# Attention and a gated MLP on one core: buffers of x and of its parts shared by both halves of the MLP, g loaded into the place of its low part

## The chip, the cores and the metric

The kernel runs on one core of a Trainium2 chip. The metric is the device time of one execution in microseconds (us); the median of three runs is given, and one further execution was profiled. TensorE does the matrix products, VectorE (DVE), ScalarE (ACT) and GpSimd (POOL) the elementwise work, SyncE (SP) issues the transfers between HBM and the on-chip memory SBUF. TensorE adds up in PSUM, of which the kernel has four tiles, `ps0` to `ps3`.

## What is computed

Attention with rotary positions, then two gated layers. Four batches, eight heads, 576 positions, head size 64, width 512:

```
attn_out = softmax(rot(q) @ rot(k).T / 8) @ v          # 4 x 8 x 576 x 64
x = attn_out, heads side by side                       # 4 x 576 x 512

h = gelu_tanh(x @ w_in)                                # 4 x 576 x 1024
u, v = h[..., :512], h[..., 512:]
v_n = layer_norm(v) * g_ln                             # over the 512
v_s = einsum('ts,bsd->btd', w_sg, v_n) + b_sg[:, None]
g = u * v_s
x2 = x + g @ w_out

gate = sigmoid(causal_conv5(x2, conv_w))               # 5 taps along the positions, zeros ahead
out = (gate * (x2 @ w_val)) @ w_out2
```

The results must be as exact as float32 products. So each operand of a product is split into a high part (a rounded copy) and a low part (what the rounding left), and a product is the sum of three: high x high, high x low, low x high.

## The kernel before

**Stages.** Attention runs over 16 pairs of heads (0 to 289 us). Each pair leaves its unnormalised result in a scratch array `xu_d` in HBM and the reciprocals of its sums in `r_d`. Then comes the first half of the MLP, `part_a(b)` for the batches 0 to 3, some 41 us each (289 to 454 us), and then the second half (454 to 615 us).

**First half.** `x_prep(b)` makes x of a batch, in four tiles of 128 of the 512 columns (x is kept transposed, 128 columns by 576 positions). For each tile: a load of `xu_d`, a load of the broadcast reciprocals into `rb` (two DMAs), the product on GpSimd, a store of x to `x_d`, a rounded copy to `XH` on ScalarE, and the low part `XL` = x - `XH` on VectorE. `XH` and `XL` exist once (four tiles each), so the copies for batch b + 1 wait until TensorE has read those of batch b. `part_a(b)` then runs three products on TensorE: x by w_in for v (L607, 60 matmuls, 13.7 us), x by w_in for u (L646, 96 matmuls, 12.7 us; `u_unit`), and the mixing along the positions with w_sg (L660 and L663, 14.8 us; `g_unit`). `XH` and `XL` are read by the first two, so what prepares the next batch has the third as its time. `g_unit` ends with `vs` on VectorE (L667), a product with u on GpSimd, and a store of g to `g_d` in HBM.

`x_prep(0)` and the loading of w_sg use two tiles `xs0`, `xs1`. `x_prep(1)` to `x_prep(3)` use four, `xs0`, `xs1` and the two `gst` tiles, one for each of the four tiles of x.

**Weights.** Weights arrive as 64-bit floats. `weight64` loads one (512 KB, into the single raw buffer `wr0` from the first half on), takes a step on ScalarE (L281) and four on VectorE (L282 to L288) to make float32 `wf`, a rounded copy on ScalarE and a low part on GpSimd. Twelve of these (w_out, w_val, w_out2, four each: `wo`, `wv`, `wq`) are spread over the first half. The last is in place at 460.4 us.

**Second half.** When the first half's last work is done (`opened["2"]`, `close_a`), its pools are closed and the second half's tiles are put in their place. `load_g(b)` brings g of a batch back: a load into a staging tile (`gst`, for two tiles of batch 1 the `ob` tiles), a rounded copy to `gh` on ScalarE, the low part `gl` on VectorE. There are two sets `gh0`/`gl0` and `gh1`/`gl1`, for even and odd batches. `load_g(0)` runs in the first half, `load_g(1)` after `close_a`. `x2_part(b)`: for each of four tiles a load of x from `x_d` into one of four `x2` tiles (four zero columns and 576), 24 matmuls g by w_out (L728), an addition on VectorE into the `x2` tile (L734, this also frees the PSUM tile), a rounded copy `xh` on ScalarE, the low part `xl` on GpSimd, and the convolution `gt`: one ScalarE step (L743), four VectorE steps (L746), a sigmoid on ScalarE (L748). `val_part(b)`: four times 24 matmuls x2 by w_val (L761), a product with the gate on VectorE (L768), the split into `yh` and `yl`. `out_part(b)`: y by w_out2 (L790) and the output. The order on TensorE is `x2_part(0)`, half of `x2_part(1)`, `val_part(0)`, the other half of `x2_part(1)`, `out_part(0)`, half of `x2_part(2)`, and so on. Products take the PSUM tiles in turn, so a product can start when the result four before it has been read.

**What sets the order.** The program is first written as a list of tasks with an engine, an estimated duration and the tiles read and written (`Plan.add`); `Plan.order` then makes a schedule from these estimates (earliest possible, the most urgent first), and instructions are issued in that order. TensorE's order is fixed. On each engine, and in SyncE's queue, instructions run strictly in order: one that waits holds all behind it.

Of the kernel before, what the change touches and what calls it, by code (L numbers as in the profile page):

```python
# [155 lines left out]
def mixer_kernel(ctx: ExitStack, tc: tile.TileContext, qk, v, vrem, cs, w_in, g_ln, w_sgT, b_sg,  # L156
# [148 lines left out]
    def weights_a():  # L305
# [11 lines left out]
        for k in range(5):  # L317
            xs = XS[k % 2]
# [369 lines left out]

    def load_g(b):
        j = b % 2  # L690
        op = [opened["2" if j else "1"]]
        for k in range(4):
            y = k % 2
            spare = b == 1 and k > 1

            def st(y=y, spare=spare):
                return T["ob"][y].rearrange("p a b -> p (a b)")[:, 0:S] if spare else T["gst"][y]
            ks = ("ob" if spare else "gst", y)
            dma(290, lambda q, k=k, st=st: q.dma_start(out=st(), in_=g_d[b][128 * k:128 * k + 128, :]),
                [("g_d", b, k)], [ks], after=op)  # L700
            split(lambda k=k: T["gh"][j][:, k], lambda k=k: T["gl_"][j][:, k], st, S, [ks],
                  ("G", j, k, "h"), ("G", j, k, "l"), "D")
# [6 lines left out]
    def x2_part(b, dds=range(4)):  # L709
        j = b % 2  # L710
        op2 = [opened["2"]]
        for dd in dds:
            dc = slice(128 * dd, 128 * dd + 128)
            y = nx[0] % 4
            nx[0] += 1
            kx = ("x2", y)

            def x2(y=y):
                return T["x2"][y]
            dma(290, lambda q, dd=dd, x2=x2: q.dma_start(out=x2()[:, 4:S + 4], in_=x_d[4 * b + dd]),  # L720
                [("x_d", 4 * b + dd)], [kx], after=op2)
# [8 lines left out]
            ps, kp = unit(24 * PASS, mm, [("G", j, k, m) for k in range(4) for m in "hl"] + [(f"wo{k}", m) for k in range(4) for m in "hl"])  # L730

            def mid(x2=x2):
# [3 lines left out]
                [kp, ("x2z",)], [kx], after=op2)  # L736
# [107 lines left out]
    def close_a():  # L844
# [3 lines left out]
        T["gh"].append(p2.tile([128, 4, S], F32R, name="gh1"))  # L848
        T["gl_"].append(p2.tile([128, 4, S], F32R, name="gl1"))
# [6 lines left out]
        T["x2"] = [p2.tile([128, S + 4], F32, name=f"x2{j}") for j in range(4)]  # L856
# [7 lines left out]
    add("Pool", 0.3, lambda: [nc.gpsimd.memset(T["x2"][j][:, 0:4], 0.0) for j in range(4)], w=[("x2z",)], after=[opened["2"]])  # L864
# [74 lines left out]
```

## Time and profile before

| | us |
|---|---|
| median of three runs | 616.0 |
| lowest, highest | 615.06, 620.21 |
| the profiled execution | 616.6 |
| its span in the trace | 614.8 |
| TensorE busy | 579.0 (94%) |
| VectorE busy | 396.1 (64%) |
| ScalarE busy | 275.3 (45%) |
| GpSimd busy | 299.2 (49%) |
| granted TensorE clock, mean | 0.997 |

Times in the trace count from the span's start. The span is from the first to the last instruction; 1.8 us of the execution lie around it. TensorE's busy time is the union of its matmuls, whose ends are modelled. The trace names a wait by the instruction that ended it; "issue" stands where it names none.

### The profile page before, as it was taken

To read this page: it belongs to the slowest core of one execution; us is meant where nothing else is said; L and a number is where in the kernel's file an instruction comes from. 1 tells how busy PE (TensorE), PEld (TensorE's weight loads), DVE (VectorE), ACT (ScalarE), POOL (GpSimd) and SP (SyncE) were. 2 spreads that over 40 slices of the span, in tenths; PEclk is the share of its full clock that TensorE was granted. 3 is DMA by queue.
4 is the path that set the end of the run, shared out by engine and by line. 5 is a ranking of instruction groups with operands and counts; after the bars stand their busy time and mean duration, and the time that the engine had idled before them with its cause. 6 is when DMAs were issued, how large, how long until landed. Compare 5 with 4: busy or idle time off the path is not lost.

```text
span 614.8 us, 12049 instructions
## 1 busy us (share of the span) xinstructions
PE 579.0 (94%) x4648; PEld 465.5 (76%) x4648; DVE 396.1 (64%) x580; ACT 275.3 (45%) x447; POOL 299.2 (49%) x240
## 2 busy tenths in 40 slices
PE   1689999999999999999999999999998899999997
PEld 1456565666666566665899998998998889989985
DVE  5767765676666686771465666776457998938730
ACT  2426555555555556665441432624316554333321
POOL 6646565555555455556777745745544222201200
PEclk9989999999999999999999999999999999999999
DMA  7523644444444623665647246222144243130002
GB/s 254 166 83 86 182 144 123 124 118 128 122 100 130 190 74 111 194 198 141 197 143 278 76 154 218 79 97 85 38 150 155 78 138 124 39 125 2 35 31 90
DMA packets 54873, 76.80 MB, mean 125 GB/s; under 512 B 26528, under 2 KB 30624, under 8 KB 54816
## 3 DMA queue, kind: packets, MB, share of 16 engines
q1 hardware_dynamic: 54592, 76.03, 40.5%
q8 instruction: 36, 0.59, 0.4%
q14 instruction: 21, 0.17, 0.1%
q10 hardware_dynamic: 224, 0.00, 0.0%
HBM read 55.33 MB, written 18.95 MB: 121 GB/s over the span
## 4 chain that ended last, share of the span: by engine, by line
PE 80%; DVE 9%; DMA 7%; SPq 1%; POOL 1%; issue 1%; ACT 1%; DVEq 0%; ACTq 0%; POOLq 0%
PE ps L424 10%; PE ps L607 9%; PE ps L455 9%; PE ps L646 8%; PE ps L660 8%; PE ps L790 8%; PE ps L761 7%; PE ps L728 5%; PE ps L382 5%; PE ps L491 4%; DMA raw<-qk 3%; PE ps L432 3%; DVE mx L384 3%; DVE raw L236 2%; DVE gt L746 2%; PE ps L465 1%
## 5 line engine op out<-in xcount | busy, mean ns | idle before, releaser
L384 DVE TENSOR_REDUCE mx<-ps 128x2 f32<-128x576 f32 x128 | 96.2, 756 | 67.1 <-PE ps L382 66.5
L437 ACT ACTIVATE e<-ps 128x576 f32<-128x576 f32 x144 | 87.2, 648 | 70.0 <-PE ps L424 44.4
L455 PE MATMUL ps<-e,vm 128*64 128x288 f32 x512 | 77.6, 425 | 0.0
L382 PE MATMUL ps<-kh,qp 64*128 64x288 f32 x256 | 50.4, 393 | 24.1 <-ACT kh L240 13.0
L237 POOL TENSOR_TENSOR xl<-x,xh 128x576 fp32r<-128x576 f32 x16 | 27.9, 1751 | 88.1 <-ACT xh L240 79.4
L382 PEld LDWEIGHTS ps<-kh,qp 64*128 64x128 f32 x256 | 25.5, 197 | 56.6 <-DVE mx L384 23.1
L237 POOL TENSOR_TENSOR ac<-e,e 128x576 f32<-128x576 f32 x32 | 48.8, 1545 | 28.8 <-PE ps L491 27.0
L746 DVE SCALAR_TENSOR_TENSOR gt<-x,cw,gt 128x576 f32<-128x576 f32 x64 | 59.4, 967 | 3.5 <-ACT gt L743 3.2
L236 DVE TENSOR_TENSOR raw<-raw,cst 128x576 f32<-128x576 f32 x60 | 52.4, 888 | 8.1 <-DMA raw<-qk 8.1
L660 PE MATMUL ps<-s_h,vn 128*128 128x288 f32 x256 | 56.0, 294 | 0.0
L237 POOL TENSOR_TENSOR raw<-raw 128x576 f32<-128x576 f32 x30 | 43.4, 1446 | 16.8 <-DVE raw L236 15.1
L455 PEld LDWEIGHTS ps<-e,vm 128*64 128x64 f32 x512 | 31.3, 137 | 22.9 <-issue 6.0
L424 PE MATMUL ps<-qh,kh 64*128 64x288 f32 x256 | 42.0, 322 | 2.8 <-DVE mn L392 1.8
L660 PEld LDWEIGHTS ps<-s_h,vn 128*128 128x128 f32 x256 | 42.8, 188 | 0.0
L424 PE MATMUL ps<-mr,one_r 64*128 64x288 f32 x256 | 40.1, 302 | 0.1
L424 PE MATMUL ps<-qh,kl 64*128 64x288 f32 x256 | 39.4, 301 | 0.6 <-DVE kl L236 0.6
L761 PE MATMUL ps<-xh,wh_v 128*128 128x288 f32 x128 | 37.8, 295 | 1.8 <-DVE x L734 1.8
L424 PE MATMUL ps<-ql,kh 64*128 64x288 f32 x256 | 39.3, 300 | 0.0
L728 PE MATMUL ps<-gh,wh_o 128*128 128x288 f32 x128 | 37.7, 295 | 1.0 <-issue 1.0
L761 PE MATMUL ps<-xl,wh_v 128*128 128x288 f32 x128 | 37.8, 295 | 0.7 <-POOL xl L237 0.7
L237 POOL TENSOR_TENSOR vs<-vs,u 128x576 f32<-128x576 f32 x16 | 26.0, 1624 | 24.4 <-DVE vs L667 24.2
L660 PE MATMUL ps<-s_l,vn 128*128 128x288 f32 x128 | 37.8, 295 | 0.0
(145 smaller groups left out, 1576.2 us busy)
## 6 DMA issues: line engine op xcount, KB each, us to landing
raw<-qk SPq DMA_DIRECT2D x32, 576.0 KB, 4.5
xu_d<-xu SPq DMA_DIRECT2D x32, 144.0 KB, 3.4
rb<-r_d SPq DMA_DIRECT2D x32, 144.0 KB, 3.4
g_d<-vs SPq DMA_DIRECT2D x16, 288.0 KB, 2.7
x<-x_d SPq DMA_DIRECT2D x16, 288.0 KB, 2.9
vm<-v SPq DMA_DIRECT2D x16, 256.0 KB, 3.0
wr<-w_in SPq DMA_DIRECT2D x8, 512.0 KB, 5.5
wr<-w_out SPq DMA_DIRECT2D x8, 512.0 KB, 3.9
```

The costliest lines, as they stand in the source:

```text
L236: return add("DVE", dve(n), lambda: nc.vector.tensor_tensor(out_(), a(), b(), op), r, w, lock=True)
L237: return add("Pool", pool(n), lambda: nc.gpsimd.tensor_tensor(out_(), a(), b(), op), r, w, lock=True)
L382: nc.tensor.matmul(ps[:, h, 0:HALF], QP[j2][rows, c], kh[rows, cols], start=True, stop=True)
L384: add("DVE", 0.76, lambda: nc.vector.tensor_reduce(out=MX[j2][:, hk, :, c], in_=ps[:, :, 0:HALF], axis=AX.X, op=ALU.max), [kps], [("mx", j ...
L424: nc.tensor.matmul(ps[:, h, 0:HALF], x[rows, keys] if o < 3 else x[rows], y[rows, cols], start=o == 0, stop=o == 3)
L437: add("Act", 0.62, lambda: nc.scalar.activation(E[n], ps[:, :, 0:HALF], AF.Exp), [kps], [("e", n)])
L455: nc.tensor.matmul(pv[64 * hf:64 * hf + 64, h, 0:HALF], VM[j2][:, j, h], E[EU[i, us[hf]]][:, h], start=j == 0, stop=False, skip_group_chec ...
L607: nc.tensor.matmul(ps[:, y], X[p][:, k, o:o + 128], Wm[q][:, k, 512:1024], start=k == z == 0, stop=k == 3 and z == 2)
L660: nc.tensor.matmul(ps[:, hf, 0:HALF], VN()[p][:, k, dc], SG[q][:, k, cols], start=k == z == 0, stop=False)
L728: nc.tensor.matmul(ps[:, hf, 0:HALF], w2("o", p)[:, k, dc], (T["gh"], T["gl_"])[q][j][:, k, cols], start=k == z == 0, stop=k == 3 and z == 2)
L746: add("DVE", dve(S) + 0.05, lambda dd=dd, m=m, x2=x2, gt=gt: nc.vector.scalar_tensor_tensor(gt(), x2()[:, m:m + S], cw[:, 5 * dd + m:5 * d ...
L761: nc.tensor.matmul(ps[:, hf, 0:HALF], w2("v", p)[:, k, dc], (T["xh2"], T["xl2"])[q][j][:, k, cols], start=k == z == 0, stop=k == 3 and z == 2)
```

## The change

Four things are changed.

- `XH` and `XL`, the two tiles `xs` and the two tiles `rb` move from the first half's pool to the pool that lives through the whole kernel. `xs` and `rb` get four more columns in front, filled with zeros at the start on GpSimd; the first half uses columns 4 to 579.
- `x_prep(1)` to `x_prep(3)` use two tiles, `xs0` and `xs1`, each twice, as `x_prep(0)` does. The `gst` tiles are gone.
- `XH` and `XL` are `gh1` and `gl1` in the second half. `load_g` has no staging tile: g is loaded into the place of its own low part (`gl0`, or `XL`), copied from there to the high part, and the subtraction writes over its own input. It waits only for the tiles (and for `opened["1"]`), not for `close_a`.
- The four `x2` tiles are `xs0`, `xs1`, `rb0`, `rb1`. Their loads and the addition on VectorE no longer wait for `close_a`; the zero columns are not filled again.

```diff
+    XH = const.tile([128, 4, S], F32R, name="XH")
+    XL = const.tile([128, 4, S], F32R, name="XL")
+    XS = tiles(const, "xs", 2, [128, 4 + S], F32)
+    RB = tiles(const, "rb", 2, [128, 4 + S], F32)
-    XH = pA.tile([128, 4, S], F32R, name="XH")
-    XL = pA.tile([128, 4, S], F32R, name="XL")
-    XS = tiles(pA, "xs", 2, [128, S], F32)
-    RB = tiles(pA, "rb", 2, [128, S], F32)
...
+            for t in (*XS, *RB):
+                nc.gpsimd.memset(t[:, 0:4], 0.0)
...
     def x_prep(b):
-            y = hp if b else hp % 2
-            rb = RB[hp % 2]
-            kx = ("xs", y) if y < 2 else ("gst", y - 2)
-            op = [opened["1"]] if y > 1 else [at[13]]
+            y = hp % 2
+            rb = RB[hp % 2][:, 4:]
+            kx = ("xs", y)
+            op = [at[13]]
...
+    def gk(j, k, m):
+        return ("X", k, m) if j else ("G", k, m)
     def load_g(b):
         j = b % 2
-        op = [opened["2" if j else "1"]]
         for k in range(4):
-            y = k % 2
-            spare = b == 1 and k > 1
-            def st(y=y, spare=spare):
-                return T["ob"][y].rearrange("p a b -> p (a b)")[:, 0:S] if spare else T["gst"][y]
-            ks = ("ob" if spare else "gst", y)
-            dma(290, lambda q, k=k, st=st: q.dma_start(out=st(), in_=g_d[b][128 * k:128 * k + 128, :]),
-                [("g_d", b, k)], [ks], after=op)
-            split(lambda k=k: T["gh"][j][:, k], lambda k=k: T["gl_"][j][:, k], st, S, [ks],
-                  ("G", j, k, "h"), ("G", j, k, "l"), "D")
+            def g(k=k):
+                return T["gl_"][j][:, k].bitcast(F32)
+            kh, kl = gk(j, k, "h"), gk(j, k, "l")
+            dma(290, lambda q, k=k, g=g: q.dma_start(out=g(), in_=g_d[b][128 * k:128 * k + 128, :]), [("g_d", b, k)], [kl],
+                after=[opened["1"]])
+            acopy(lambda k=k: T["gh"][j][:, k], g, S, [kl], [kh])
+            tt("D", lambda k=k: T["gl_"][j][:, k], g, lambda k=k: T["gh"][j][:, k].bitcast(F32), ALU.subtract, S, [kh], [kl])
...
     def x2_part(b, dds=range(4)):
-        op2 = [opened["2"]]
-            y = nx[0] % 4
+            x2t, kx = ((XS[0], ("xs", 0)), (XS[1], ("xs", 1)), (RB[0], ("rb", 0)), (RB[1], ("rb", 1)))[nx[0] % 4]
...
             dma(290, lambda q, dd=dd, x2=x2: q.dma_start(out=x2()[:, 4:S + 4], in_=x_d[4 * b + dd]),
-                [("x_d", 4 * b + dd)], [kx], after=op2)
+                [("x_d", 4 * b + dd)], [kx])
...
-                [kp, ("x2z",)], [kx], after=op2)
+                [kp], [kx])
...
-        T["gst"] = [p1.tile([128, S], F32, name=f"gst{j}") for j in range(2)]
+        T["gh"] = [p1.tile([128, 4, S], F32R, name="gh0"), XH]
+        T["gl_"] = [p1.tile([128, 4, S], F32R, name="gl0"), XL]
...
-    add("Pool", 0.3, lambda: [nc.gpsimd.memset(T["x2"][j][:, 0:4], 0.0) for j in range(4)], w=[("x2z",)], after=[opened["2"]])
```

The planner makes a new order from this. TensorE's order and everything up to the middle of the first block of the MLP stay as they are. Three places follow.

VectorE, at the end of the block of batch 1 (after the weight conversion that stands there); `XL` rows are the low parts of x for batch 2, `vs` rows the `g_unit` of batch 1. Before:

```order
L236 TENSOR_TENSOR XL_136<-xs0_137,XH_135 128x576
L236 TENSOR_TENSOR XL_136<-xs1_138,XH_135 128x576
L236 TENSOR_TENSOR XL_136<-gst0_3322,XH_135 128x576
L236 TENSOR_TENSOR XL_136<-gst1_3323,XH_135 128x576
L667 SCALAR_TENSOR_TENSOR vs0_3333<-ps2_123,gsb_125,bsb_126 128x576
```

And now:

```order
L238 TENSOR_TENSOR XL_132<-xs0_133,XH_131 128x576
L238 TENSOR_TENSOR XL_132<-xs1_134,XH_131 128x576
L671 SCALAR_TENSOR_TENSOR vs0_3335<-ps2_123,gsb_125,bsb_126 128x576
L671 SCALAR_TENSOR_TENSOR vs1_3336<-ps3_124,gsb_125,bsb_126 128x576
L238 TENSOR_TENSOR XL_132<-xs0_133,XH_131 128x576
L286 TENSOR_SCALAR wt0_143<-wt0_143 128x512
L238 TENSOR_TENSOR XL_132<-xs1_134,XH_131 128x576
```

The third and fourth low part moved behind two `vs` steps and one weight step; the tiles they read are the first two's, loaded anew.

SyncE, around the same place: loads of x for batch 2 (`xu_d8` to `xu_d11`). Before, all four stand early, in the block of batch 0 (`g_d0` is the store of g of batch 0):

```order
L584 DMA xs0_137<-xu_d8_77 128x576
L299 DMA wr0_141<-w_out 128x1024
L584 DMA xs1_138<-xu_d9_78 128x576
L584 DMA gst1_3323<-xu_d11_80 128x576
L584 DMA gst0_3322<-xu_d10_79 128x576
L670 DMA g_d0_117<-vs0_3333 128x576
L588 DMA rb0_139<-r_d10_111 64x576 x2
```

And now, for the third and fourth (the loads of `xu_d8` and `xu_d9` stand a few rows further ahead, between the stores of `g_d0`):

```order
L595 DMA x_d8_93<-xs0_133 128x576
L592 DMA rb0_135<-r_d10_111 64x576 x2
L595 DMA x_d9_94<-xs1_134 128x576
L592 DMA rb1_136<-r_d11_112 64x576 x2
L674 DMA g_d0_117<-vs1_3336 128x576
L702 DMA gl0_3325<-g_d0_117 128x576
L303 DMA wr0_141<-w_out 128x1024
L303 DMA wr0_141<-w_val 128x1024
L588 DMA xs0_133<-xu_d10_79 128x576
L588 DMA xs1_134<-xu_d11_80 128x576
```

The loads of `xu_d10` and `xu_d11` moved behind the weights `wo3` and `wv0`, into the tiles that the first two leave.

VectorE, where the second half begins: `wt`, `wf` are steps of the last weight, `vs1_...<-ps3` the last step of the first half, `gl1` or `XL_132<-XL_132` the low parts of g of batch 1, L734 (L735 now) the additions of `x2_part(0)`, L746 (L747 now) convolution steps. Before:

```order
L667 SCALAR_TENSOR_TENSOR vs1_3334<-ps3_124,gsb_125,bsb_126 128x576
L282 TENSOR_SCALAR wt0_143<-wt0_143 128x512
L284 TENSOR_SCALAR wt0_143<-wt0_143 128x512
L286 SCALAR_TENSOR_TENSOR wt0_143<-wr0_141,wt0_143 128x512
L288 SCALAR_TENSOR_TENSOR wf0_142<-wr0_141,wt0_143 128x512
L236 TENSOR_TENSOR gl1_4848<-gst0_3322,gh1_4847 128x576
L236 TENSOR_TENSOR gl1_4848<-gst1_3323,gh1_4847 128x576
L236 TENSOR_TENSOR gl1_4848<-ob0_4865,gh1_4847 128x576
L236 TENSOR_TENSOR gl1_4848<-ob1_4866,gh1_4847 128x576
L734 TENSOR_TENSOR x20_4861<-ps0_121,x20_4861 128x576
L734 TENSOR_TENSOR x21_4862<-ps1_122,x21_4862 128x576
L734 TENSOR_TENSOR x22_4863<-ps2_123,x22_4863 128x576
```

And now:

```order
L238 TENSOR_TENSOR XL_132<-XL_132,XH_131 128x576
L671 SCALAR_TENSOR_TENSOR vs0_3335<-ps2_123,gsb_125,bsb_126 128x576
L238 TENSOR_TENSOR XL_132<-XL_132,XH_131 128x576 x2
L671 SCALAR_TENSOR_TENSOR vs1_3336<-ps3_124,gsb_125,bsb_126 128x576
L286 TENSOR_SCALAR wt0_143<-wt0_143 128x512
L288 TENSOR_SCALAR wt0_143<-wt0_143 128x512
L735 TENSOR_TENSOR xs0_133<-ps0_121,xs0_133 128x576
L290 SCALAR_TENSOR_TENSOR wt0_143<-wr0_141,wt0_143 128x512
L292 SCALAR_TENSOR_TENSOR wf0_142<-wr0_141,wt0_143 128x512
L735 TENSOR_TENSOR xs1_134<-ps1_122,xs1_134 128x576
L747 SCALAR_TENSOR_TENSOR gt0_4871<-xs0_133,cw_127,gt0_4871 128x576
L735 TENSOR_TENSOR rb0_135<-ps2_123,rb0_135 128x576
```

The low parts of g moved ahead of the last `vs` and the last weight, the first addition ahead of the end of that weight, and convolution steps stand between the additions.

## Rows read from the trace of the kernel before

**Rows 1.** TensorE's waits from 289 us on: waiting, releaser, us in total, times, longest.

```profile
PE ps L761 <- DVE x L734: 1.8, 1, 1.8
PE ps L728 <- issue: 1.0, 1, 1.0
PE ps L761 <- POOL xl L237: 0.7, 1, 0.7
```

**Rows 2.** Stretch, us, busy us (instructions) of PE PEld DVE ACT POOL, clock, DMA.

```profile
330.00:371.00 41.00, 41.00 (x268) 38.61 (x267) 25.54 (x40) 15.45 (x24) 27.40 (x22) 1.00 0.42 143
466.50:490.00 23.50, 20.07 (x148) 19.47 (x147) 22.77 (x26) 14.27 (x23) 10.47 (x6) 1.00 0.19 64
490.00:610.00 120.00, 120.00 (x744) 110.15 (x742) 77.92 (x112) 44.20 (x76) 17.43 (x10) 1.00 0.23 74
```

**Rows 3.** TensorE's timeline: start, us, what (idle before it and releaser in brackets).

```profile
466.38 0.29 PE L728 MATMUL ps<-gh,wl_o 128*128 128x288 f32 x1
```

**Rows 4.** The chain that ended last, in order of time: start, us, what.

```profile
371.56 13.65 PE ps L607 x60
...
483.32 6.62 PE ps L761 x48
489.94 6.36 PE ps L728 x48
```

**Rows 5.** VectorE's timeline, 454 to 481 us (columns as in rows 3).

```profile
454.05 0.82 DVE L667 SCALAR_TENSOR_TENSOR vs<-ps,gsb,bsb 128x576 f32<-128x576 f32 x1 [2.89 <-PE ps L663]
454.86 0.43 DVE L282 TENSOR_SCALAR wt<-wt 128x512 f32<-128x512 f32 x1
...
457.69 0.69 DVE L288 SCALAR_TENSOR_TENSOR wf<-wr,wt 128x512 int32<-128x512 int32 x1
...
466.79 0.76 DVE L734 TENSOR_TENSOR x<-ps,x 128x576 f32<-128x576 f32 x1 [1.17 <-DMA x<-x_d]
467.95 2.08 DVE L734 TENSOR_TENSOR x<-ps,x 128x576 f32<-128x576 f32 x3 [0.40 <-issue]
469.95 10.52 DVE L746 SCALAR_TENSOR_TENSOR gt<-x,cw,gt 128x576 f32<-128x576 f32 x9
```

**Rows 6.** GpSimd's timeline (columns as in rows 3).

```profile
9.79 5.05 POOL L237 TENSOR_TENSOR raw<-raw,cst 128x576 f32<-128x576 f32 x3 [5.38 <-DMA raw<-qk]
...
459.12 1.29 POOL L237 TENSOR_TENSOR wl_q<-wf,wh_q 128x512 fp32r<-128x512 f32 x1 [2.54 <-ACT wh_q L240]
...
469.05 7.16 POOL L237 TENSOR_TENSOR xl<-x,xh 128x576 fp32r<-128x576 f32 x4 [8.39 <-ACT xh L240]
```

**Rows 7.** SyncE: an issue of transfers, and a wait of its queue (400 to 500 us).

```profile
461.28 1.85 SPq L720 DMA_DIRECT2D x<-x_d  x4
SPq L670 <- POOL vs L237: 32.7, 8, 7.4
```

**Rows 8.** By tile, 455 to 500 us: durations min/median/max in ns.

```profile
L746 DVE SCALAR_TENSOR_TENSOR gt<-x,cw,gt x19: 800/806/2009, 469.9 to 497.2; 128x576 f32<-128x576 f32 x19
L237 POOL TENSOR_TENSOR xl<-x,xh x8: 1427/1910/1978, 469.1 to 498.1; 128x576 fp32r<-128x576 f32 x8
```

**Rows 9.** VectorE's timeline where batch 1 ends, low parts of x.

```profile
359.35 1.42 DVE L236 TENSOR_TENSOR XL<-gst,XH 128x576 fp32r<-128x576 f32 x2
...
364.19 0.82 DVE L667 SCALAR_TENSOR_TENSOR vs<-ps,gsb,bsb 128x576 f32<-128x576 f32 x1 [0.79 <-PE ps L663]
```

**Rows 10.** Tile xs, 285 to 500 us (ns; landing in us); weight loads, median us to landing.

```profile
L237 POOL TENSOR_TENSOR xs<-xs,rb x6: 1437/1600/1946, 298.7 to 366.9; 128x576 f32<-128x576 f32 x6
L240 ACT CAST XH<-xs x6: 665/672/681, 316.2 to 399.1; 128x576 fp32r<-128x576 f32 x6
L236 DVE TENSOR_TENSOR XL<-xs,XH x6: 751/754/757, 316.9 to 399.9; 128x576 fp32r<-128x576 f32 x6
DMA to landing us min/median/max: 2.6/3.5/5.6
wr<-w_out SPq DMA_DIRECT2D x8, 512.0 KB, 3.9
```

More of the change, by code (lines that the diff above doesn't have):

```diff
@@ L317, in weights_a @@
         for k in range(5):
-            xs = XS[k % 2]
+            xs = XS[k % 2][:, 4:]
             def ld(q, k=k, xs=xs):
@@ L576, in x_prep @@
             i = 4 * b + hp
-            y = hp if b else hp % 2
-            rb = RB[hp % 2]
-            kx = ("xs", y) if y < 2 else ("gst", y - 2)
-            op = [opened["1"]] if y > 1 else [at[13]]
+            y = hp % 2
+            rb = RB[hp % 2][:, 4:]
+            kx = ("xs", y)
+            op = [at[13]]
             def xs(y=y):
-                return XS[y] if y < 2 else T["gst"][y - 2]
+                return XS[y][:, 4:]
             dma(290, lambda q, xs=xs, i=i: q.dma_start(out=xs(), in_=xu_d[i]), [("xu_d", i)], [kx], after=op)
@@ L710, in x2_part, with x2 @@
         j = b % 2
-        op2 = [opened["2"]]
         for dd in dds:
             dc = slice(128 * dd, 128 * dd + 128)
-            y = nx[0] % 4
+            x2t, kx = ((XS[0], ("xs", 0)), (XS[1], ("xs", 1)), (RB[0], ("rb", 0)), (RB[1], ("rb", 1)))[nx[0] % 4]
             nx[0] += 1
-            kx = ("x2", y)
-            def x2(y=y):
-                return T["x2"][y]
+            def x2(x2t=x2t):
+                return x2t
             dma(290, lambda q, dd=dd, x2=x2: q.dma_start(out=x2()[:, 4:S + 4], in_=x_d[4 * b + dd]),
-                [("x_d", 4 * b + dd)], [kx], after=op2)
+                [("x_d", 4 * b + dd)], [kx])
             def mm(ps, dc=dc):
@@ L729, in mm @@
                                              start=k == z == 0, stop=k == 3 and z == 2)
-            ps, kp = unit(24 * PASS, mm, [("G", j, k, m) for k in range(4) for m in "hl"] + [(f"wo{k}", m) for k in range(4) for m in "hl"])
+            ps, kp = unit(24 * PASS, mm, [gk(j, k, m) for k in range(4) for m in "hl"] + [(f"wo{k}", m) for k in range(4) for m in "hl"])
             def mid(x2=x2):
@@ L743, in x2_part @@
             add("Act", act(S) + 0.09, lambda dd=dd, x2=x2, gt=gt: nc.scalar.activation(
-                gt(), x2()[:, 0:S], AF.Copy, scale=cw[:, 5 * dd:5 * dd + 1]), [kx, ("x2z",), ("cw",)], [kg])
+                gt(), x2()[:, 0:S], AF.Copy, scale=cw[:, 5 * dd:5 * dd + 1]), [kx, ("consts",), ("cw",)], [kg])
             for m in range(1, 5):
@@ L816, in close_att @@
             T["wl" + nm] = p1.tile([128, 4, DM], F32R, name=f"wl_{nm}")
-        T["gh"] = [p1.tile([128, 4, S], F32R, name="gh0")]
-        T["gl_"] = [p1.tile([128, 4, S], F32R, name="gl0")]
-        T["gst"] = [p1.tile([128, S], F32, name=f"gst{j}") for j in range(2)]
+        T["gh"] = [p1.tile([128, 4, S], F32R, name="gh0"), XH]
+        T["gl_"] = [p1.tile([128, 4, S], F32R, name="gl0"), XL]
         pa2 = stA2.enter_context(tc.tile_pool(name="pA2", side="right", bufs=1))
@@ L847, in close_a @@
         p2 = ctx.enter_context(tc.tile_pool(name="pB2", bufs=1))
-        T["gh"].append(p2.tile([128, 4, S], F32R, name="gh1"))
-        T["gl_"].append(p2.tile([128, 4, S], F32R, name="gl1"))
         for nm in ("xh2", "xl2"):
@@ L855, in close_a @@
         T["yr"] = [p2.tile([128, 2, 4, 128], F32R, name=f"yr{j}") for j in range(2)]
-        T["x2"] = [p2.tile([128, S + 4], F32, name=f"x2{j}") for j in range(4)]
         T["ob"] = [p2.tile([128, 2, 512], F32, name=f"ob{j}") for j in range(2)]
```

## Prediction

> **What bounds the kernel now.** I first read where TensorE waits, because it is busy 94% of the span. From 289 us to the end it waits three times only: 1.8 us for VectorE's `x`, 1.0 us for something unnamed, 0.7 us for GpSimd's `xl` [rows 1]. The table by stretch says the same from the other side: TensorE is busy 41.00 of 41.00 us in a block of the first MLP half and 120.00 of 120.00 us from 490 to 610, but only 20.07 of 23.50 us between 466.5 and 490 [rows 2]. So a change to the MLP can gain only in those 23.5 us, and it can lose wherever it makes TensorE wait elsewhere.
>
> How large that gain can be at most: the last matmul of `x2_part(0)` starts at 466.38 [rows 3] and the next would follow 0.13 later, at 466.51. From there to the end of `val_part(0)` stand six products of 24 matmuls; two of them take 6.36 us in the chain [rows 4], so 3.18 each and 19.08 together: 485.59 without any wait. In fact the chain has 483.32 + 6.62 = 489.94 [rows 4]. The ceiling is 4.35 us, of which 3.5 are the three waits of [rows 1] and the rest is restart.
>
> Why it waits there: the first half ends with the last weight. VectorE finishes its conversion at 457.69 + 0.69, ScalarE rounds it, GpSimd subtracts from 459.12 to 460.41 [rows 5, 6], and only then are the buffers of the second half handed out. The four `x` tiles are loaded from 461.28 on [rows 7], and VectorE's additions of `x` run at 466.79 and from 467.95 to 470.03 [rows 5], although the first of the four products had been ready since 466.51 − 3 × 3.18 = 456.97. Everything behind them is late by some 9 us: GpSimd's `xl` (469.05) [rows 6], VectorE's convolution (469.95, without a break until 480.47) [rows 5].
>
> **The change part by part.**
>
> *Buffers of x.* The `x2` tiles now are XS and RB, which exist all along. Their loads stand in SyncE's queue ahead of the last `g_d` stores, behind the end of `x_prep(3)`, so they land tens of microseconds before 457. The additions then follow TensorE: 457.3 (VectorE has a 1.54 us weight step up to there), 460.4, 463.6 and, since VectorE's queue is in order, 466.7 for the last, which ends at 467.4.
>
> *g in place of its low part, in XL and XH.* Loads, copies and subtractions stay 4 per batch, of the same size (ScalarE 0.67, VectorE 0.75, as for the parts of x [rows 10]), so they add no work. For batch 1 they move from behind the last weight to the 14.8 us in which TensorE runs `g_unit`, after `u_unit` releases XH and XL at about 439.1 (four products of 3.18 and the 14.7 of `g_unit` before 466.51). Four loads issued from 439.3 land by about 445 (four such `x` loads issued from 461.28 were all there by 467.95 [rows 5, 7]), and the four subtractions now stand between VectorE's `vs` steps and the last two weights. Their price: 4 × 0.75 = 3.0 us on VectorE, most of it in its pauses (2.89 us ahead of the last `vs` alone [rows 5]); what does not fit pushes the last conversion from 458.38 to about 459.4, and GpSimd's last weight step from 460.41 to about 461.5. So the second half's own buffers open 1.1 us later than before, but less hangs on them.
>
> *The convolution.* ScalarE starts `gt` at 461.5 and `xh` at 462.3; GpSimd's four `xl` run from 463.1 to 470.3. TensorE goes straight from 466.51 into batch 1 (ps0 is free since 458) and needs `xl` at 472.87: the wait of 0.7 us is gone with 2.6 us to spare. VectorE does two of its convolution steps before 467.4; eight follow before the gate product of the first `val` result. A step takes 0.81 us alone and up to 2.01 beside GpSimd, whose `xl` then takes 1.91 instead of 1.43 [rows 8]. With two held up by 1.1 and six at 0.8 they end at 475.9, and the first `val` product ends at 476.05. So the first late addition of batch 1, which frees ps0, ends at 477.8, before TensorE asks for it at 479.23: the wait of 1.8 us is gone too. The second one stands behind four more steps, of which one is held up by the next `xl`: it ends at 483.2, and TensorE asks for ps1 at 482.41. **One wait of 0.8 us is left.** Gain: 4.35 − 0.8 = **3.5 us**.
>
> What stands behind the rows on [rows 8] is stated by the Trainium skill, "SBUF — State Buffer", section "Who interferes with whom": a VectorE instruction with two SBUF inputs and a GpSimd instruction that reads SBUF exclude each other for a whole instruction. It speaks against this change, which brings subtractions under GpSimd's `vs` products; the trace agrees (2.01 against 0.81 us). Without such exclusion the left-over wait would be nil and the gain 4.3; with it, 3.5.
>
> *x_prep with two buffers instead of four.* Before, four tiles were loaded, multiplied and stored early, so that at the end of `u_unit` (356.72) four copies and four subtractions ran back to back, done at 359.35 + 1.42 = 360.77 [rows 9]. Now the second pair can only be loaded when VectorE's subtraction has released the first. Worked for block 1: subtraction of the first tile at 358.0, load issued at 358.8 (as SyncE did before for the next batch) and landed 3.5 us later, 362.3 [rows 10]; GpSimd has the `vs` product until 363.1, then two multiplications of 1.60 [rows 10], to 364.7 and 366.3; copy 0.67, subtraction behind `vs` of 364.19: 366.1; the last pair 367.0 and 367.7, with one weight step between. TensorE needs them at 371.56 [rows 4]: 3.9 us to spare, three times. The store to `x_d` and the loads of `rb` lie in SyncE's queue behind; nothing waits for them in this block. Cost on the path: **0**. If the cover is gone, each microsecond beyond 3.9 costs one at each of three block starts.
>
> *Small things.* Four GpSimd fills of four columns move to the start, where GpSimd is idle for 5.38 us before its first product, since a transfer is what it waits for [rows 6]: 0; only past 5.38 us would they delay it. `g` of batches 2 and 3 now loads only when TensorE has read the old values (466.5 and about 493), but is needed at 504 and 546: 0.
>
> **Sum.** 614.8 − 3.5 = 611.3 us of span; the profiled execution took 616.6, 1.8 more than its span, so 613.1. The median of the three runs, 616.0, lies 0.6 below that execution; against it the forecast is 616.0 − 3.5 = **612.5 us**, 0.6% faster. A measurement of this kernel can tell about 1% from no change, so this counts as "same".
>
> **Rivals.**
> *The wait only moves (616).* If VectorE is not ahead after all, TensorE stops at ps1 instead of ps0. It costs one for one from 482.41 on; the whole gain is lost when the second addition ends at 486.8, 3.6 us after my 483.2. That takes three more convolution steps held to 2.0 us, or buffers that open 3.6 us later since the last weight is late. For it: VectorE has no pause from 469.95 to 490 and is the engine that the longest wait names [rows 1, 5]. Against: its first addition moves 9 us forward and GpSimd's interfering products with it. 0.17.
>
> *Two buffers are too few (slower).* The chain subtraction, load, product, copy, subtraction must fit into `g_unit`'s 14.8 us. The slowest `xs` load seen took 5.6 us, 2.1 more than my 3.5 [rows 10]; that alone stays inside 3.9. If SyncE's queue, in order and with a weight load that waits for VectorE just ahead of the pair, holds it 3 us more, TensorE waits 1.2 us three times and the gain is spent: the kernel is slower than before from 5.1 us of lateness per block, 619 at 6.1. For it: one queue carries all this, and its waits for GpSimd's `vs` were up to 7.4 us [rows 7]. Against: the weight just ahead must be converted by 358.0; its load, after the conversion before it (about 345.4 in the new order), takes 3.9 [rows 10], ScalarE comes to it behind `u` at 351.1, and VectorE's four steps take 3.5 (454.86 to 458.38 [rows 5]) and a few tenths of waiting: 355.3. 0.10.
>
> *All of the 4.35 us (611.7).* The left-over 0.8 rests on one step held up by `xl`; where GpSimd starts a little later, nothing is left. This lies within the forecast's own range.
>
> **How the numbers follow.** Forecast (gain 2 to 4.35): 0.70; the wait moves (gain under 2): 0.17; X late: 0.10; other, as an effect of addresses or of the first half's shifted weight order: 0.03. Range: below, the ceiling of 4.35 and the scatter of the lower runs (615.06 is 0.9 below the median) give 610.8; above, the case without a gain, 616.5. Forecast's own range: 611.2 to 614.2. Faster by over 1% would need 6.2 us, more than the ceiling: 0.03. Slower by over 1% needs X to be late by (6.2 + 3.5) / 3 + 3.9 = 7.1 us in each block: 0.06. Within 1%: 0.91.
>
> **What would show it.** Right: from 289 us on TensorE waits once for under 1.5 us, at the last product of `val_part(0)`, with VectorE's addition as releaser; VectorE's first addition stands at about 457; 490 to the end is as dense as before, 3.5 us earlier. Wrong: a wait of `X Wm` products at a block start with `XL` or the `xs` load ahead of it; the last weight's GpSimd step well after 461.5; an addition into ps1 ending later than 484.

## The result and the profile after

The changed kernel takes 612.9 us (median), the kernel before 616.0 in the same comparison. The ratio is **0.9919, 95% interval 0.9894 to 0.9944**: 0.8% faster. That is the forecast case (612.5 us, 0.6% faster), and within 1%. The ratio's interval means 3.4 to 6.5 us on 616.0; the medians lie 3.1 us apart, the profiled spans, 614.8 and 611.1, 3.7. Single executions of one kernel scatter by more than that (608.3 to 618.2 for the changed one), so where the time went is read from the traces. Page of the changed kernel, span and busy times:

```profile
span 611.1 us, 12019 instructions
PE 580.7 (95%) x4648; PEld 467.1 (76%) x4648; DVE 389.2 (64%) x580; ACT 276.0 (45%) x447; POOL 301.1 (49%) x240
```

The list of TensorE's waits from 280 us on is now empty; the three of [rows 1] are gone (0.25 us that the list does not name is taken up under `short_xl`). The table by stretch (columns as in [rows 2]) shows the same for the 23.5 us in which TensorE was busy for 20.07 before:

```profile
330.00:371.00 41.00, 41.00 (x267) 38.36 (x266) 26.28 (x43) 16.56 (x27) 27.38 (x22) 1.00 0.55 182
466.50:490.00 23.50, 23.50 (x178) 23.28 (x177) 20.16 (x25) 13.96 (x24) 8.05 (x5) 1.00 0.32 102
```

Since lines were added, L607, L660, L728, L734, L746, L761, L768 and L790 of before are L611, L664, L729, L735, L747, L762, L769 and L791 after. The chain after (start, us, what), the products that answer to [rows 4] and a few more:

```profile
330.98 13.94 PE ps L611 x60
...
372.47 13.94 PE ps L611 x60
...
455.45 19.09 PE ps L729 x144
474.53 12.97 PE ps L762 x96
487.50 6.36 PE ps L729 x48
493.86 10.92 PE ps L791 x48
...
530.21 13.62 PE ps L791 x60
```

and of the kernel before, products by `w_h` and by `wh_q` that no group ahead shows:

```profile
330.36 13.65 PE ps L607 x60
...
496.30 11.20 PE ps L790 x48
532.94 13.94 PE ps L790 x60
```

The first product after the transition stands at 487.50 instead of 489.94 [rows 4], only 2.44 us earlier, although TensorE no longer waits. Two things that I had not worked out lie beside the transition: each block of the first half has become 0.29 us longer (L611: 13.94 against 13.65), and each output product shorter (L791: 10.92 against 11.20 for 48 matmuls, 13.62 against 13.94 for 60). I cut the trace of every kernel at the starts of matmuls: the first of the first block, the first of `x2_part(0)`, the first behind `val_part(0)`, and the end. These sums, in us, answer most of what follows (`only_x` and the rest are the kernels of the experiments below; each was profiled in one execution):

| kernel | four blocks | transition | rest | all three |
|---|---|---|---|---|
| before | 164.90 | 35.98 | 125.00 | 325.88 |
| changed | 166.08 | 32.05 | 123.72 | 321.85 |
| `only_x` | 164.91 | 36.73 | 123.68 | 325.32 |
| `only_g` | 164.91 | 33.18 | 125.00 | 323.09 |
| `two_buf` | 164.90 | 34.66 | 125.01 | 324.57 |
| `one_buf` | 205.20 | 31.81 | 123.71 | 360.72 |
| `pad_w` | 164.90 | 32.05 | 123.70 | 320.65 |
| `pad_w256` | 166.11 | 32.05 | 123.73 | 321.89 |
| `pad_w64` | 166.41 | 32.05 | 123.72 | 322.18 |
| `pad_before` | 164.91 | 35.26 | 123.70 | 323.87 |
| `short_xl` | 166.11 | 31.81 | 123.70 | 321.62 |

So from before to after: +1.18 in the blocks, -3.93 in the transition, -1.28 in the rest, -4.03 in all (and the first block began 0.31 later, which leaves the 3.7 of the two spans). What stands ahead of the first block, the attention, is left out of the table: over these eleven executions it ended anywhere from 287.2 to 293.2 us, in no order of the kernels. One execution of each kernel was profiled, so no run shows whether the change moves that end as well, nor how much of the scatter of the measured times it is.

### The profile page after: what moved, and what is told of

It is laid out like the page before. It is cut to its first block, busy times and chain, and to the rows that moved or that the text cites. A ratio compares the mean times of both kernels' runs of the same rounds, so it can differ in the third digit from the quotient of the medians.

```text
span 611.1 us, 12019 instructions
## 1 busy us (share of the span) xinstructions
PE 580.7 (95%) x4648; PEld 467.1 (76%) x4648; DVE 389.2 (64%) x580; ACT 276.0 (45%) x447; POOL 301.1 (49%) x240
## 4 chain that ended last, share of the span: by engine, by line
PE 84%; DVE 7%; DMA 5%; SPq 1%; issue 1%; ACT 1%; POOL 0%; DVEq 0%; ACTq 0%; POOLq 0%
PE ps L428 9%; PE ps L611 9%; PE ps L459 9%; PE ps L762 8%; PE ps L650 8%; PE ps L729 8%; PE ps L664 8%; PE ps L791 8%; PE ps L386 5%; PE ps L495 4%; PE ps L436 3%; DVE mx L388 3%; DVE raw L238 2%; DMA raw<-qk 2%; PE ps L667 1%; DMA rc<-ss 1%
## 5 line engine op out<-in xcount | busy, mean ns | idle before, releaser
L459 PE MATMUL ps<-e,vm 128*64 128x288 f32 x512 | 79.0, 431 | 0.0
L664 PE MATMUL ps<-s_h,vn 128*128 128x288 f32 x256 | 56.0, 294 | 0.0
L238 DVE TENSOR_TENSOR raw<-raw,cst 128x576 f32<-128x576 f32 x60 | 48.7, 826 | 6.9 <-DMA raw<-qk 6.9
L459 PEld LDWEIGHTS ps<-e,vm 128*64 128x64 f32 x512 | 31.8, 139 | 23.5 <-issue 7.0
L664 PEld LDWEIGHTS ps<-s_h,vn 128*128 128x128 f32 x256 | 42.7, 188 | 0.0
L239 POOL TENSOR_TENSOR kl<-raw,kh 128x576 fp32r<-128x576 f32 x15 | 22.6, 1508 | 31.6 <-ACT kh L242 30.8
L650 PE MATMUL ps<-XH,w_l 128*128 128x288 f32 x128 | 37.8, 295 | 0.0
L762 PE MATMUL ps<-xh,wh_v 128*128 128x288 f32 x128 | 37.8, 295 | 0.0
L762 PE MATMUL ps<-xh,wl_v 128*128 128x288 f32 x128 | 37.8, 295 | 0.0
L664 PE MATMUL ps<-s_l,vn 128*128 128x288 f32 x128 | 37.7, 295 | 0.0
L650 PE MATMUL ps<-XL,w_h 128*128 128x288 f32 x128 | 37.7, 294 | 0.0
```

The costliest lines, as they stand in the source:

```text
L238: return add("DVE", dve(n), lambda: nc.vector.tensor_tensor(out_(), a(), b(), op), r, w, lock=True)
L239: return add("Pool", pool(n), lambda: nc.gpsimd.tensor_tensor(out_(), a(), b(), op), r, w, lock=True)
L459: nc.tensor.matmul(pv[64 * hf:64 * hf + 64, h, 0:HALF], VM[j2][:, j, h], E[EU[i, us[hf]]][:, h], start=j == 0, stop=False, skip_group_chec ...
L650: nc.tensor.matmul(ps[:, hf, 0:HALF], Wm[p][:, k, dc], X[q][:, k, cols], start=k == z == 0, stop=k == 3 and z == 2)
L664: nc.tensor.matmul(ps[:, hf, 0:HALF], VN()[p][:, k, dc], SG[q][:, k, cols], start=k == z == 0, stop=False)
L762: nc.tensor.matmul(ps[:, hf, 0:HALF], w2("v", p)[:, k, dc], (T["xh2"], T["xl2"])[q][j][:, k, cols], start=k == z == 0, stop=k == 3 and z == 2)
```

## The experiments

The theory: TensorE's waits in the transition go because both loads, of x and of g, no longer stand behind the last weight. Rivals: the loads of x are all of it; or the buffers of `x_prep` are a loss that hides part of it. A second question came from the chain: what makes L611 and L791 change speed.

### Only the buffers of x2 (`only_x`)

The kernel before, with `XS` and `RB` as constant tiles used by `x2_part`; `load_g` and `x_prep` as before.

```diff
-            y = nx[0] % 4
-            kx = ("x2", y)
+            x2t, kx = ((XS[0], ("xs", 0)), (XS[1], ("xs", 1)), (RB[0], ("rb", 0)), (RB[1], ("rb", 1)))[nx[0] % 4]
...
-                [("x_d", 4 * b + dd)], [kx], after=op2)
+                [("x_d", 4 * b + dd)], [kx])
```

> One part of the change alone: x2_part works in the four buffers of x and r, so the loads of x stand ahead of the end of the first half; g still goes through gst and ob, after it, and x_prep keeps four buffers. Theory: both early loads are needed. The first additions come at about 457, 460, 463.6 and 466.7, but the four subtractions of g's low part (block 1) stand behind the fourth of them on VectorE, so they end at 470.3 (0.75 us each) to 473 (1.43 each beside POOL's xl), and the first product of x2_part(1), which reads them and is asked for at 466.5, waits 3.8 to 6.5 us; the later waits (0.69 and 1.76) go, since their work is then early. Against the 3.43 us of waits before that is 0.4 to 3 us worse. The distances of the tiles (theory A of the paddings) are 0 for both 512-column products, which gives 1.26 back: 615.2 to 617.9, centre 616. Rival: the loads of x are the whole effect; then no wait is left and the time is 616.0 - 4.1 - 1.3 = 610.6.

Measured: ratio to before 1.0022 (0.9997 to 1.0048), that is 617.4 us on 616.0, not told apart from the kernel before. The additions are early, but now TensorE's wait is for g: 2.8 us in two pieces, where I had expected 3.8 to 6.5 in one. Its list of waits, and VectorE's timeline (columns as in [rows 5]):

```profile
PE ps L729 <- DVE gl L237: 2.8, 2, 1.5
```

```profile
460.66 0.76 DVE L735 TENSOR_TENSOR xs<-ps,xs 128x576 f32<-128x576 f32 x1 [0.41 <-PE ps L729]
...
470.20 0.76 DVE L735 TENSOR_TENSOR rb<-ps,rb 128x576 f32<-128x576 f32 x1 [1.70 <-PE ps L729]
470.87 1.58 DVE L237 TENSOR_TENSOR gl<-gst,gh 128x576 fp32r<-128x576 f32 x2
472.37 2.63 DVE L237 TENSOR_TENSOR gl<-ob,gh 128x576 fp32r<-128x576 f32 x2
474.92 3.00 DVE L747 SCALAR_TENSOR_TENSOR gt<-xs,cw,gt 128x576 f32<-128x576 f32 x4
```

The four subtractions of g end at 475, behind the fourth addition, as expected. TensorE starts again after each of them in turn and stands twice for 1.5 us at most. Six products took 24.0 us where 19.1 is the length without waits, though the waits are only 2.8. The table by stretch tells a part of why:

```profile
471.00:475.00 4.00, 1.94 (x8) 1.47 (x9) 4.00 (x5) 2.11 (x4) 1.78 (x2) 0.88 0.46 149
475.00:478.00 3.00, 3.00 (x16) 3.00 (x16) 3.00 (x5) 2.71 (x4) 0.00 (x0) 0.60 0.02 6
478.00:481.30 3.30, 3.30 (x27) 3.30 (x27) 3.30 (x5) 0.63 (x2) 0.00 (x0) 1.00 0.32 89
```

TensorE was busy for 1.94 of 4.00 us, and then the granted clock was 0.60 over three microseconds (partly at the lower of its two levels, 1.2 GHz), in which 16 matmuls ran where 22 to 23 go at 0.133 us each: 0.9 us. The other 1.2 lie in longer distances between the matmuls around the two waits. The rival (no wait left, 610.6) is out, by the ratio and by the waits: the loads of x alone are worth nothing, as the work on g takes their place.

### Only g in its own place (`only_g`)

The kernel before, with `XH` and `XL` as constant tiles and the new `load_g`; `x2` has its own four tiles, opened by `close_a`.

```diff
-        op = [opened["2" if j else "1"]]
...
+                after=[opened["1"]])
...
-        T["gh"] = [p1.tile([128, 4, S], F32R, name="gh0")]
...
+        T["gh"] = [p1.tile([128, 4, S], F32R, name="gh0"), XH]
```

> The other part alone: g is loaded into XL's place and its high part into XH, early; x2_part has its own four tiles, opened at the end of the first half, and x_prep keeps four buffers. Theory: no subtraction of g is left in the transition and the loads of x are no longer behind two loads into ob; they are issued about 460.2 instead of 461.3 and the first addition comes at about 465.5, before TensorE asks for its buffer at 466.5, so the wait of 0.98 goes; the second addition of x2_part(1) ends about 484.2 where TensorE asks at 482.4, so one wait of about 1.8 is left of 3.43: 614.4 us. Both 512-column products keep their distances of before (0 and 128 mod 256), so L607 takes 13.65 and L790 13.94: no change from those. Rival: the loads of x are the whole effect, then all three waits stay and the time is 616.0.

Measured: ratio 0.9943 (0.9916 to 0.997), transition 33.18 us. One wait is left (`PE ps L761 <- DVE x L734: 1.1, 1, 1.1` in its list), where I expected 1.8. VectorE's timeline:

```profile
465.62 1.49 DVE L734 TENSOR_TENSOR x<-ps,x 128x576 f32<-128x576 f32 x2 [5.09 <-DMA x<-x_d]
...
481.59 0.74 DVE L734 TENSOR_TENSOR x<-ps,x 128x576 f32<-128x576 f32 x1
...
483.71 0.75 DVE L734 TENSOR_TENSOR x<-ps,x 128x576 f32<-128x576 f32 x1
```

VectorE stands idle for 5.09 us until x has landed; its first addition comes at 465.6, which is 463.8 in the time of before, since the transition began at 455.67 here and at 453.80 there. I had expected 465.5, which was 1.7 too late. The addition that TensorE waits for is the first late one, into ps0: it ends at 482.33, and TensorE's next product starts at 482.39. I had expected the second, into ps1, to be the one that counts; behind the wait at ps0 that one (ended at 484.46) is in time. So the first wait goes as expected, the place of the last was wrong, and the price 0.7 less. In all, g is the larger part: 2.8 us of the 3.9 against the profile of before. The early loads of x add 1.13 to it, but only on top of it. The two parts are not a sum: 36.73 and 33.18 alone, 32.05 together, from 35.98.

### Only two buffers in `x_prep` (`two_buf`)

The kernel before with this one edit:

```diff
-            y = hp if b else hp % 2
+            y = hp % 2
```

> The kernel before with one edit: x_prep uses two buffers of x for every block instead of four (gst stays for g alone). Theory: a block's XL is ready about 3 us before its first product also with two buffers (368 against 371.6), so the time stays at 616.0 and no wait stands ahead of L607. Rival (two are too few): the third and fourth load come behind the release of the first two, XL ends after 371.6, and each of the three later blocks loses up to 3 us: 619 to 625.

Measured: ratio 0.9978 (0.9945 to 1.0012), four blocks 164.90 us as before to a hundredth. No wait stands at a block's start; two buffers cost nothing. In the transition, which this edit leaves alone, two of the three waits stand as before:

```profile
PE ps L761 <- DVE x L734: 1.8, 1, 1.8
PE ps L761 <- POOL xl L237: 0.6, 1, 0.6
```

The unnamed one of 1.0 is not there. In `pad_before`, whose transition is also that of before, it was 0.3:

```profile
PE ps L730 <- issue: 0.3, 1, 0.3
```

The first of the four loads of x took 5.4 us from issue to landing in the profile of before, 4.7 in `pad_before` and 4.1 in `two_buf`. So this wait depends on when x lands in one execution: the transition of before took 35.98, 35.26 and 34.66 us in the three, 35.3 in the mean, and against that mean 0.7 of the 3.9 us gained were the profiled execution's own.

### One buffer of x (`one_buf`)

The changed kernel with this one edit:

```diff
-            y = hp % 2
+            y = 0
```

> The changed kernel with one buffer of x in x_prep instead of two (the two of r stay). It shows where the spare time of 3.1 us ends. Theory: a pair must then be loaded (2.6 to 3.5 us), multiplied (1.4), stored and split before the next is loaded, about 6.5 us a pair; only the first is ready when u_part frees XH, so the fourth XL comes about 6 to 8 us after TensorE asks for it in each of the three later blocks: 612.9 + 18 to 24, about 632 us, with waits of DVE XL ahead of L611. Rival (x_prep has more slack than that, since work of the block before covers it): under 2 us a block, below 619.

Measured: 654.4 us in one run; the blocks take 205.20 us, 39.1 more than in the changed kernel, 13 for each of the three later blocks. The pair's cycle is longer than I put it: for the second block the last two products on GpSimd follow one another by 8.58 us (335.76 to 344.34), not 6.5, and I had expected about 632 us.

```profile
PE ps L611 <- ACT XH L242: 28.9, 6, 7.9
```

```profile
335.76 1.87 POOL L239 TENSOR_TENSOR xs<-xs,rb 128x576 f32<-128x576 f32 x1 [3.48 <-DMA xs<-xu_d]
344.34 1.40 POOL L239 TENSOR_TENSOR xs<-xs,rb 128x576 f32<-128x576 f32 x1
```

```profile
333.40:347.00 13.60, 4.14 (x12) 2.30 (x11) 6.73 (x10) 4.45 (x7) 5.85 (x4) 0.66 0.81 263
347.00:360.70 13.70, 13.70 (x51) 10.81 (x50) 8.69 (x22) 5.64 (x8) 6.66 (x6) 0.84 0.48 138
```

The waits are 28.9 of the 39.1. Of the other 10.2, about 8.5 are matmuls that follow one another more slowly; the granted clock was 0.66 in the stretch in which TensorE stood and 0.84 in the one behind. The remaining 1.7 lie in the first intervals after the waits. So the rival "two buffers are too few" had the right mechanism and the wrong count: one buffer fewer turns 3 us to spare into 13 us of loss a block.

### Where the 512-column products get their speed (`pad_w`, `pad_w256`, `pad_w64`, `pad_before`)

The starts of the matmuls of L611 follow one another by 232 ns after the change and by 227 before; for L791 it is 227 after and 232 to 233 before. The matmuls of 288 columns keep their 132.5. What the change moved are addresses. Counted in bytes per partition, the program puts `XH` at 0 (mod 256) from `w_h` before and at 128 after; `yh` is at 128 from `wh_q` before and at 0 after, and the low parts stand likewise. An unused tile in the changed kernel moves them:

```diff
+    pA.tile([128, 32], F32, name="pad")
     w_h = pA.tile([128, 4, 1024], F32R, name="w_h")
```

is `pad_w`; 64 instead of 32 elements make `pad_w256`, 16 `pad_w64`. In `pad_before` the pad is the last constant tile of the kernel before, so that `w_h` and `XH` move together and `yh` moves against `wh_q`.

> The changed kernel with one unused tile of 128 bytes per partition put ahead of w_h, so that the first weights and s_h, s_l lie 128 bytes further on; nothing else. In the profile of the change, the 60 matmuls of 512 columns of a block's first product (L611) take 13.94 us where they took 13.65, and those of the output product (L791) 13.62 where they took 13.94. Theory A: a 512-column matmul is slower (232 instead of 227 ns from one start to the next) where its stationary and its moving tile lie at an odd multiple of 128 bytes from one another; in the change XH lies at 128 (mod 256) from w_h, before it lay at 0, and for yh and wh_q it is the other way round. By A this kernel has both at 0: L611 goes back to 13.65 in four blocks (1.16 us in all), L791 stays at 13.62, the span is 609.9 and the time 611.7, 0.7% below the kernel before. Rival B: the two speeds belong to where the products stand in the program or to the pool of XH, not to the distance; then L611 stays at 13.94 and the time at 612.9.

> The control for the paddings: as the changed kernel, with 256 bytes ahead of w_h, so that XH lies at 128 (mod 256) from w_h as it does in the change. Theory A: L611 stays at 13.94 and the span at 611.1. Rival (any move of w_h away from where it lay helps, or the added tile itself): 13.65 and 609.9.

> As the changed kernel, with 64 bytes ahead of w_h: XH lies at 64 (mod 256) from w_h. Theory A says nothing sure of 64: if what counts is whether the two lie at the same place within 128 bytes, L611 is off by more than at 128 (over 13.94); if it is a question of the 128-byte step alone, it lies at 13.65 or 13.94. Either way the other products stay, and the span is 609.9 to about 612.

> The kernel before with an unused tile of 128 bytes per partition as the last of the constants: w_h and XH, which lie in one pool, move together, and yh, yl, yr move against wh_q. Theory A (the distance of stationary and moving tile decides): L607 stays at 13.65, L790 goes to 10.92, 13.62, 5.48 and 19.08 from 11.20, 13.94, 5.60 and 19.62, so the time falls by 1.26 us to 614.8 (0.2%), with the three waits of the transition as they are (0.98, 0.69, 1.76). Rival B (an absolute address, or the place in the program): L607 gets slower or L790 stays.

Measured, by the chains. `pad_w` (L612 and L792 are the two products):

```profile
334.61 13.65 PE ps L612 x60
...
532.96 13.62 PE ps L792 x60
```

`pad_w256`, the same program with the pad twice as long:

```profile
330.93 13.94 PE ps L612 x60
...
530.17 13.62 PE ps L792 x60
```

`pad_w64`:

```profile
370.63 13.99 PE ps L612 x60
```

and `pad_before` (L609 and L792):

```profile
333.02 13.66 PE ps L609 x60
...
534.61 13.62 PE ps L792 x60
```

At a distance of 0 a product is fast, at 128 slow, wherever the two tiles lie: `pad_before` moved both `w_h` and `XH` by 128 bytes and L609 stayed fast, while L792 became fast. At 64 it is slowest (13.99). So the rival, that the speed belongs to the place in the program or to the pool, is out. The column of the blocks takes two values, 164.90 and 166.1 (166.41 at 64; `one_buf`, with its waits, aside), that of the rest 125.00 and 123.70, and each kernel takes the one that its distances say, `only_x` and `only_g` too. Why the distance matters, no run here shows.

`pad_w` has the change's transition and both products fast. Its measured ratio to before is 0.9901 (0.9866 to 0.9936), against 0.9919 for the change. These intervals overlap; the table tells them apart, 320.65 against 321.85 us. Its own profiled span was 613.8, since its first block began at 293.2. `pad_before` has the ratio 0.9985 (0.9961 to 1.0008) to before, not told apart from it, where 0.998 was expected. `pad_w256` and `pad_w64` ran once each, at 612.8 and 611.2 us; that the one with the slowest blocks has the lower time shows that single times settle nothing here.

### The last wait, and what GpSimd costs VectorE (`short_xl`)

In the change, 96 matmuls of `val_part(0)` take 12.97 us where 12.72 is usual. TensorE's timeline, with starts 0.13 apart elsewhere, has it at one place:

```profile
483.78 0.29 PE L762 MATMUL ps<-xh,wl_v 128*128 128x288 f32 x1
484.05 0.40 PE L762 MATMUL ps<-xh,wh_v 128*128 128x288 f32 x1
484.29 0.29 PE L762 MATMUL ps<-xl,wh_v 128*128 128x288 f32 x1
```

The second of these lines begins the last product of `val_part(0)`, and VectorE's addition into its PSUM tile ends at 483.99:

```profile
477.82 0.76 DVE L769 TENSOR_TENSOR gt<-ps,gt 128x576 f32<-128x576 f32 x1 [1.64 <-PE ps L762]
478.50 0.75 DVE L735 TENSOR_TENSOR xs<-ps,xs 128x576 f32<-128x576 f32 x1
479.16 4.17 DVE L747 SCALAR_TENSOR_TENSOR gt<-rb,cw,gt 128x576 f32<-128x576 f32 x4
483.25 0.74 DVE L735 TENSOR_TENSOR xs<-ps,xs 128x576 f32<-128x576 f32 x1
```

The edit: the subtraction of the first `xl` of batch 1, which GpSimd runs from 480.70 to 482.72 beside those four steps, is cut to 64 of its 576 columns; the rest of that low part is set to zero, so the kernel leaves it out of the results of batch 1.

```diff
-            split(lambda dd=dd: T["xh2"][j][:, dd], lambda dd=dd: T["xl2"][j][:, dd], mid, S, [kx],
-                  ("X2", j, dd, "h"), ("X2", j, dd, "l"))
+            cut = b == 1 and dd == 0
+            n = 64 if cut else S
+            acopy(lambda dd=dd: T["xh2"][j][:, dd], mid, S, [kx], [("X2", j, dd, "h")])
+            tt("P", lambda dd=dd, n=n: T["xl2"][j][:, dd, 0:n], lambda mid=mid, n=n: mid()[:, 0:n],
+               lambda dd=dd, n=n: T["xh2"][j][:, dd, 0:n].bitcast(F32), ALU.subtract, S, [kx, ("X2", j, dd, "h")], [("X2", j, dd, "l")])
...
+    add("Pool", 0.6, lambda: nc.gpsimd.memset(T["xl2"][1][:, 0].bitcast(F32), 0.0), w=[("X2", 1, 0, "l")], after=[opened["2"]])
```

> The changed kernel, with the subtraction of xl on POOL for the first tile of x2_part(1) cut to 64 of 576 columns (the rest of that low part is set to zero ahead of x2_part, so the values of block 1 lack it). In the profile of the change, that subtraction runs 480.70 to 482.72 beside four gt steps of VectorE (479.16 to 483.33, 1.04 us each, where 0.73 from start to start stands without POOL, 473.19 to 476.2), and TensorE stands 0.25 us at 483.9 until the addition behind them ends at 483.99. Theory: POOL's subtraction costs VectorE the 4.17 - 4 x 0.73 = 1.25 us; with 64 columns the four steps end about 1.1 us earlier, the addition at about 482.8 (counted from 455.45, the start of x2_part(0): 27.4 instead of 28.5), TensorE's 0.25 is gone, and L762's first 96 products take 12.72 instead of 12.97. Rival: the four steps are slow by themselves or by ACT's work; then they keep 4.17 and 12.97.

Measured: 612.7 us in one run. VectorE of `short_xl`:

```profile
479.25 3.06 DVE L750 SCALAR_TENSOR_TENSOR gt<-rb,cw,gt 128x576 f32<-128x576 f32 x4
482.24 0.74 DVE L735 TENSOR_TENSOR xs<-ps,xs 128x576 f32<-128x576 f32 x1
```

The four steps take 3.06 instead of 4.17 us, the addition stands 1.1 earlier (the start of `x2_part(0)` differs by 0.1 only), and the transition falls from 32.05 to 31.81: TensorE's last 0.25 us is gone. So that subtraction on GpSimd costs VectorE 1.1 us, and this alone makes the wait.

## Why the prediction was right, and where it was off

**The waits.** Right. In the change the last matmul of `x2_part(0)` starts at 467.88, before at 466.38 [rows 3], so everything is 1.50 later; in the time of before, VectorE's four additions stand at 457.2, 460.3, 463.5 and 466.7. I had 457.3, 460.4, 463.6 and 466.7. VectorE's timeline after, first and fourth addition, and what follows:

```profile
458.67 0.76 DVE L735 TENSOR_TENSOR xs<-ps,xs 128x576 f32<-128x576 f32 x1 [0.16 <-PE ps L729]
...
468.21 0.76 DVE L735 TENSOR_TENSOR rb<-ps,rb 128x576 f32<-128x576 f32 x1 [1.70 <-PE ps L729]
468.89 4.38 DVE L747 SCALAR_TENSOR_TENSOR gt<-xs,cw,gt 128x576 f32<-128x576 f32 x4
...
475.38 0.81 DVE L747 SCALAR_TENSOR_TENSOR gt<-xs,cw,gt 128x576 f32<-128x576 f32 x1
```

**The last weight.** Right: forecast 461.5; GpSimd ends it at 462.86, in the time of before at 461.4.

```profile
461.56 1.30 POOL L239 TENSOR_TENSOR wl_q<-wf,wh_q 128x512 fp32r<-128x512 f32 x1 [3.33 <-ACT wh_q L242]
```

**The left-over wait.** Right in its place and cause, wrong in size: 0.25 us, not 0.8. The mis-sized term is the second late addition: it ends at 482.5 in the time of before, not 483.2, and TensorE asks for ps1 at 482.4, as I had it. The first late addition ends at 477.75, and I had 477.8, so the surplus lies between the two. There my own terms, three steps of 0.81, one of 2.01 and an addition of 0.75, give 483.0, not the 483.2 that I wrote; and a step starts 0.73 us after the one before it, where I took its whole length, which is most of the rest. One of the four steps was held up, as forecast. The eight steps ahead of them also ended earlier, at 474.7 instead of 475.9, in part by the same 0.73, in part since only one of them was held up where I had two; that changed nothing, since VectorE then stood 1.64 us for the first product of `val_part(0)`. So the transition gained almost the whole ceiling. By the Trainium skill ("SBUF — State Buffer", "Who interferes with whom") a VectorE instruction with two SBUF inputs and a GpSimd one that reads SBUF exclude each other; `short_xl` agrees, with 1.1 us for one such meeting.

**The ceiling.** 4.35 us was nearly right for the profile of before (35.98 to 31.81 is 4.2), but one of the three waits behind it, the 1.0, belongs to that execution (0, 0.3 and 1.0 in three). I took one execution's waits as the kernel's. Against the mean of the three the gain in the transition is nearer 3.3 than 3.9; that my 3.5 lies between is in part luck.

**x_prep with two buffers.** Right: nothing lost, as the four blocks of `two_buf` and `pad_w` show, 164.90 us in sum like before. In the second block XL is done at 369.36 and the next block starts at 372.47, 3.1 us to spare against 3.9 forecast:

```profile
367.05 1.64 DVE L286 TENSOR_SCALAR wt<-wt 128x512 f32<-128x512 f32 x1
368.61 0.75 DVE L238 TENSOR_TENSOR XL<-xs,XH 128x576 fp32r<-128x576 f32 x1
```

The weight step between the last two subtractions took 1.64 us, where I had left a few tenths for it; the block itself began 0.9 later.

**The density from 490 on.** Not as I put it. "As dense as before, 3.5 us earlier" held at the end (3.7) but not at the start, where 2.44 is all: the addresses gave 1.18 away in the blocks and 1.28 back in the output products. I had addresses only as "other" with 0.03, and the sum came out right because two terms that I left out cancel to 0.1 us, which is luck. With another layout of the same change, both could have had one sign.

## What to carry to other kernels

Moving one of two loads out of a crowded place can do nothing, or harm, if the other's work falls into the gap: in the transition, against the profile of before, x alone lost 0.75 us, g alone gained 2.8, both 3.9 (against the mean of the three executions of that transition: lost 1.4, gained 2.1 and 3.3). So write down the order of the waiting engine with each part by itself. When a change moves tiles, compare the interval of the matmuls that it leaves alone, line by line, before you put the whole difference down to the waits. And take a wait behind a transfer from more than one execution before it becomes a term of a sum.

## What the runs showed of the hardware

- A 512-column matmul of this kernel starts 227 ns after the one before it when its two operands' tiles lie at a multiple of 256 bytes from one another in a partition, 232 to 233 ns at 128 and 233 on average at 64 (mod 256), in all eleven kernels where TensorE does not wait and the granted clock is 1.00. Matmuls of 288 columns take 132.5 ns in each of them. Over this kernel's 240 and 216 such matmuls it is 1.2 and 1.3 us.
- A pause of TensorE cost more than itself: in `only_x` 2.8 us of waits came with 2.1 more, 0.9 of it in the three microseconds at a granted clock of 0.60, and in `one_buf` 28.9 came with 10.2 more, about 8.5 of it in slower matmuls.
- A GpSimd subtraction of 576 columns beside VectorE's convolution cost VectorE 1.1 us (`short_xl`), and itself took 2.02 us, against 1.43 for the shortest in [rows 8].
- Convolution steps of VectorE, 0.81 us long each, start 0.73 us after one another where nothing holds them up.
- The first of four loads of 288 KB that are issued one behind the other landed 4.1, 4.7 and 5.4 us after its issue in three executions whose order is the same at that place.
